# A spectral filter gated by a GEGLU block on one core: block products for slabs 12 and 13, one accumulating store, and a new opening

## The chip, the cores and the metric

The kernel runs on one core of one Trainium2 chip. Five engines take part: TensorE (PE; its weight loads are listed as PEld), VectorE (DVE), ScalarE (ACT), GpSimd (POOL) and SyncE (SP), which here issues transfers. The metric is device time in microseconds. Before the change it is 193.46 us, the median of three runs (193.43 to 193.47).

## The reference, cut to what matters

```python
x  = A_x                                  # (1, 2048, 640) bf16
xn = (x - mean(x)) / sqrt(var(x) + 1e-5)  # over the 640 columns
s  = irfft2(rfft2(xn) * (w_r + 1j * w_i)) # over rows and columns
g  = silu((gelu(xn @ w_gate) * (xn @ w_up)) @ w_down)
return x + s * g                          # w_gate, w_up: 640 x 1536; w_down: 1536 x 640
```

So two chains start from the normalized input: a two-dimensional Fourier filter and a gated feed-forward block. They meet in a product, and the input is added again.

## The kernel before, in words

The 2048 rows are held as 16 slabs of 128 rows by 640 columns (row = 16 x partition + slab), and four slabs make a group. The feed-forward block runs group by group. For each of the 12 tiles of 128 hidden columns there is a gate half (`ffn_piece` with k = 0: five matmuls into a bank psg, gelu on ACT into ge) and an up half (k = 1: five matmuls into a bank psu, a product with ge on DVE into UT). psg and psu have two banks each. Then the down projection of the group goes from UT and Wd into psg and psu again, and `gated` turns it into the gate G: a silu on ACT for groups 0, 2 and 3, a tanh on ACT and a product on DVE for group 1.

Groups 1 and 2 do the down projection with a block scheme for two slabs at a time (`product`): the two slabs and the two column halves of Wd, with the hidden tiles split into even and odd, make a 2 x 2 block product that is done in seven products of six matmuls of 320 columns rather than in eight. It needs sums of blocks of UT (`u_sum`, on DVE, into SS) and of Wd (`w_sum`, into TS), copies of partial results on ACT into snf and sums of them on DVE. Groups 0 and 3 do it plainly (`down_third`: 12 thirds of eight matmuls).

The filter runs beside it: folding of the input on DVE, two matrix stages per slab (`slab_S1`, `slab_D`), a store to DRAM and a load in another order, the product with the filter in 11 bursts (`s2_step`), a second round through DRAM, then the inverse stages per slab (`slab_S1i`, `slab_Di`) and the unfolding in groups of three slabs (`group_cs`, `group_Y`, `group_rest`). `finish` multiplies a slab by its gate, adds x and stores it: for slabs 0 to 11 a POOL transfer adds x in SBUF and SP stores, for slabs 12 to 15 DVE adds x, which `load_xt` brought.

The order is written by hand. `back` is the list of PE positions, 0 to 143: 0 to 15 are the first eight hidden tiles of group 0 in pieces, 16 to 23 its other four, 24 to 35 its down projection, and so on in 36s; 108 to 131 are the gate and up halves of group 3, 132 to 143 its down projection. `plan`, filled by `put(s, ...)`, hangs every other step behind a position. Each engine takes its instructions in the order in which they are emitted here. `gated(..., late)` with late set puts the silu behind the next piece and the product behind the one after (`put_off`, `flush`).

At the start, SP issues the loads of x (`load_x`) and of the weights (`load_w`), ACT issues those of Wg for the first six tiles. PE runs matmuls on a constant (`warm_pe`) until slab 0 is normalized (`stats`, `root_act` or `root`, `norm`) and transposed (`slab_Tparts`: chunks 0 to 2 and 3 to 4 apart, copied by DVE and by ACT).

## Time and profile before

| quantity | before |
|---|---|
| median of three runs | 193.46 us (193.43 to 193.47) |
| profiled execution | 193.65 us |
| its span, first to last instruction | 191.9 us |
| granted clock of the core | 1.000 |
| busy in the span: PE, DVE, ACT, POOL | 186.1, 150.9, 131.9, 53.9 us |
| first matmul on real data (not warm-up, not transposition) | 6.84 us |
| last matmul ends | 188.67 us |
| instructions | 4068 |

The profiled execution is one run, and its times hang together only within it; 1.75 us of its 193.65 lie outside the span. Times in rows are microseconds from the start of the span. A row of instructions reads: start, duration, engine, line, operation, what it writes and reads, count; in brackets what the engine waited for. A row of groups gives busy time and the mean of one in nanoseconds behind the bar. A row of the chain gives start, duration and work.

### The profile page before, as it was taken

The page shows a single profiled execution, that of the slowest core. Times are in us where ns is not written, and L with a number is a line of the kernel's source. Part 1 is how long each engine was busy: PE and PEld are TensorE (multiplying, and loading weights), DVE is VectorE, ACT ScalarE, POOL GpSimd, SP SyncE. Part 2 cuts the span into 40 slices and gives each one's busy share as a digit, 9 for nine tenths or more (in the row PEclk, how much of TensorE's full clock was granted, in tenths as well). Part 3 has the DMA queues.
Part 4 walks back from the last instruction along what each step waited for, and adds up shares of the span by engine and source line. Part 5 has one row for each costly group of instructions (what it writes and reads, how often), then busy time and mean ns, then how long its engine had stood idle before and what let it go on. Part 6 is the DMA issues. An engine that isn't in the chain of part 4 may idle for free.

```text
span 191.9 us, 4068 instructions
## 1 busy us (share of the span) xinstructions
PE 186.1 (97%) x1453; PEld 115.6 (60%) x1469; DVE 150.9 (79%) x364; ACT 131.9 (69%) x241; POOL 53.9 (28%) x91
## 2 busy tenths in 40 slices
PE   7999999999999999999999999999999999999993
PEld 5788854677655665566543334347775555556772
DVE  6787889899799889846978677685445898888973
ACT  4658557957878778536697878634989776876622
POOL 4458768999040200000000000002030134150400
PEclk9999999999999999999999999999999999999999
DMA  6999999948889994249996444149900084778842
GB/s 164 300 329 360 370 332 170 172 99 318 178 165 191 211 300 120 78 111 230 223 108 123 106 103 103 42 107 273 266 5 0 0 117 111 152 153 213 121 174 62
DMA packets 39700, 32.43 MB, mean 169 GB/s; under 512 B 12928, under 2 KB 37760, under 8 KB 39552
## 3 DMA queue, kind: packets, MB, share of 16 engines
q1 hardware_dynamic: 35888, 27.91, 58.6%
q0 software_dynamic: 1824, 3.28, 9.4%
q10 hardware_dynamic: 1968, 0.98, 1.9%
q8 instruction: 11, 0.18, 0.4%
q14 instruction: 9, 0.07, 0.1%
HBM read 19.03 MB, written 7.88 MB: 140 GB/s over the span
## 4 chain that ended last, share of the span: by engine, by line
PE 95%; DMA 2%; DVE 1%; issue 1%; SPq 0%; ACT 0%
PE psu L832 27%; PE psg L832 27%; PE psg L967 7%; PE psg L933 7%; PE psu L967 6%; PE psu L933 5%; PE pu L657 2%; PE pd L762 2%; PE pv L735 2%; PE pz L555 2%; PE pd L573 2%; PE px L628 2%; DMA X<-in_A_x_dram 2%; PE pt L994 1%; PE pd L575 1%
## 5 line engine op out<-in xcount | busy, mean ns | idle before, releaser
L832 PE MATMUL psu<-XG,Wu 128*128 128x512 bf16 (+2 forms) x284 | 60.4, 342 | 0.5 <-issue 0.3
L832 PE MATMUL psg<-XG,Wg 128*128 128x512 bf16 (+2 forms) x280 | 60.1, 341 | 0.6
L839 DVE TENSOR_TENSOR UT<-psu,ge 128x512 bf16<-128x512 f32 (+2 forms) x58 | 34.4, 594 | 13.6 <-PE psu L832 8.1
L837 ACT ACTIVATE ge<-psg 128x512 bf16<-128x512 f32 (+2 forms) x58 | 30.3, 523 | 21.3 <-PE psg L832 20.6
L832 PEld LDWEIGHTS <-Wu 128*128 128x128 bf16 x290 | 25.9, 98 | 20.9 <-issue 3.4
L832 PEld LDWEIGHTS <-Wg 128*128 128x128 bf16 x290 | 26.5, 98 | 18.8 <-issue 0.2
L967 PEld LDWEIGHTS <-UT 128*128 128x128 bf16 x204 | 19.1, 98 | 6.9
L813 POOL DMA_DIRECT2D VY<-in_A_x_dram x12 | 10.6, 964 | 26.2 <-ACT W L737 10.5
L713 POOL COPY vr<-VY 128x128 bf16<-128x128 bf16 x2 | 0.6, 291 | 60.2 <-DMA VY<-UDR 60.2
L644 DVE TENSOR_TENSOR RZ<-xs,W 128x960 bf16<-128x960 bf16 (+2 forms) x22 | 13.3, 647 | 4.4 <-ACT xs L640 4.4
L967 PE MATMUL psg<-Wd,UT 128*128 128x320 bf16 (+1 forms) x108 | 15.7, 290 | 0.0
L578 ACT CAST RZ<-pd 128x660 bf16<-128x660 f32 x16 | 11.3, 706 | 5.2 <-PE pd L575 5.2
L189 DVE BATCH_NORM_STATS2 st<-X 128x6 f32<-128x320 bf16 x32 | 14.0, 476 | 0.6 <-DMA X<-in_A_x_dram 0.4
L933 PEld LDWEIGHTS <-UT 128*128 128x128 bf16 x120 | 11.4, 98 | 4.8 <-issue 0.4
L967 PE MATMUL psu<-Wd,UT 128*128 128x320 bf16 (+1 forms) x96 | 13.9, 293 | 0.0
L737 ACT CAST W<-pv 128x640 bf16<-128x640 f32 x16 | 11.1, 691 | 3.1 <-PE pv L735 3.1
L763 ACT ACTIVATE W<-pd 128x640 bf16<-128x640 f32 x16 | 11.3, 706 | 1.5 <-PE pd L762 1.5
L557 ACT CAST GEN<-pz 128x640 bf16<-128x640 f32 x16 | 11.2, 698 | 1.2 <-PE pz L555 1.2
L672 ACT CAST RX<-pu 128x480 bf16<-128x480 f32 (+3 forms) x22 | 10.8, 489 | 1.1 <-DVE RX L672 0.3
L640 ACT CAST xs<-px 128x960 bf16<-128x960 f32 (+2 forms) x11 | 10.3, 933 | 0.0
L207 POOL TENSOR_TENSOR rst<-ve,mhalf 128x1 f32<-128x1 f32 (+1 forms) x6 | 5.5, 913 | 11.5 <-DVE ve L205 11.5
L933 PE MATMUL psg<-X,UT 128*128 128x320 bf16 x48 | 7.8, 300 | 0.0
(202 smaller groups left out, 302.1 us busy)
## 6 DMA issues: line engine op xcount, KB each, us to landing
ZDR<-RZ SPq DMA_DIRECT2D x16, 160.5 KB, 4.1
UDR<-RX SPq DMA_DIRECT2D x10, 240.8 KB, 3.1
B<-ZDR SPq DMA_DIRECT2D x8, 240.8 KB, 5.2
W<-UDR SPq DMA_DIRECT2D x2, 963.0 KB, 9.1
X<-in_A_x_dram SPq DMA_DIRECT2D x3, 640.0 KB, 10.3
Wd<-in_B_w_down_dram SPq DMA_DIRECT2D x1, 1920.0 KB, 14.6
VY<-in_A_x_dram POOLq DMA_DIRECT2D x12, 160.0 KB, 4.3
out_dram<-VY SPq DMA_DIRECT2D x12, 160.0 KB, 2.8
```

What stands on the lines that cost most here:

```text
L189: nc.vector.bn_stats(out=st_n[n1][:, k, :], in_=X[:, n1, 320 * k:320 * k + 320])
L557: nc.scalar.copy(out=Zt[n1], in_=pz)
L578: nc.scalar.copy(out=zd.rearrange("p c (q e) -> p c q e", e=10), in_=pd[:, :, 0:330].rearrange("p c (e q) -> p c q e", q=33))
L644: nc.vector.tensor_tensor(out=pp[-1], in0=xs, in1=WT[:, :, h0:h0 + n, l0:l0 + w], op=ALU.mult)
L672: copy(out=out, in_=src)
L737: nc.scalar.copy(out=vs, in_=pv)
L763: nc.scalar.activation(out=parts(eobuf, i, 5)[:, :, n1 - DG[i][0], :], in_=pd, func=ACT.Copy, scale=(2.0 if n1 // 4 in BY_SILU else 1.0) / ...
L832: nc.tensor.matmul(ps, lhsT=WT[:, c, t * P:(t + 1) * P], rhs=xnT[g][:, c, c0:c1_], start=(c == 0), stop=(c == 4))
L837: nc.scalar.activation(out=ges[t], in_=ps, func=ACT.Gelu_apprx_tanh)
L839: nc.vector.tensor_tensor(out=UT[:, t, c0:c1_], in0=ps, in1=ges[t], op=ALU.mult)
L933: nc.tensor.matmul(ps, lhsT=lhs[:, t, :], rhs=rhs[:, t, :], start=(t == 0 and i in (0, 1, 3)), stop=(t == 5), skip_group_check=i in (2, 4, ...
L967: nc.tensor.matmul(ph, lhsT=UT[:, t, j * P:(j + 1) * P], rhs=Wd[:, t, c0:c1_], start=(t == 0), stop=(t == NT - 1))
```

## The change: what it does

At the start: weights are loaded four tiles at a time, the first four in two parts of three and two chunks of the contraction. Wu's first load on SP stands behind a POOL write into Wu that reads a_y, and the load of slab 2 behind a POOL write that reads slab 0's statistics. The first four tiles are computed for slab 0 and then slab 1 in `ffn_quad` (four tiles of one slab share a bank, 20 matmuls of 128 columns), the others in `ffn_multi` (two tiles of two slabs share a bank). Gelu and product then work on 512 columns. The normalization and transposition of slab 0 come ahead of the second statistic of slab 1; slab 1's root moves from POOL to ACT, ahead of the table load of gelu; the second copy of the transposes of slabs 0 and 1 moves from ACT to DVE. The warm-up has 38 and 4 matmuls of 128 columns instead of 21 and 2 of 256. Statistics and constants move by some positions.

In the middle: `sb` goes from 67 to 65, so all bursts and everything counted from them, down to the unfolding, come two positions earlier.

At the end: for tiles 6 to 11 of group 3, ACT copies the up half from PSUM into UT and DVE multiplies there. Slabs 12 and 13 go through `product`, slabs 14 and 15 stay with `down_third`, in the order p0 and third (14,0), p2, p1, p4, third (14,1), p3, third (14,2), p6, p5, and the three thirds of slab 15. The last of these silus (product 5) follows its sum at once (late = 1). Slabs 12, 13 and 14 are finished whole, no longer by halves. For slab 13, x is stored to the output by SP right after its load; DVE writes the product of slab and gate over that x in SBUF, and POOL adds it to the output in DRAM with one accumulating transfer.

```diff
-    def load_w(k, t0, t1, eng=nc.sync):
+    def load_w(k, t0, t1, eng=nc.sync, c0=0, c1_=5):
         f0, f1 = t0 * P, t1 * P
-        eng.dma_start(out=(Wg, Wu)[k][:, :, f0:f1], in_=(wgv, wuv)[k][:, :, f0:f1])
+        eng.dma_start(out=(Wg, Wu)[k][:, c0:c1_, f0:f1], in_=(wgv, wuv)[k][:, c0:c1_, f0:f1])
...
     load_x(0, 1)
     load_x(1, 1)
-    load_w(1, 0, 2)
-    load_w(1, 2, 4)
-    load_x(2, 1)
-    load_w(1, 4, 6)
-    load_x(3, 1)
-    load_gu(6, 8)
-    load_x(4, 4)
-    load_gu(8, 12)
-    load_x(8, 4)
-    nc.sync.dma_start(out=Wd, in_=B_w_down.rearrange("(t p) d -> p t d", p=P))
-    load_x(12, 4)
...
     def root_act(n1):
-        rstd[n1] = c1("rst0")
+        rstd[n1] = c1("rst%d" % n1)
         nc.scalar.activation(out=rstd[n1], in_=mva[n1 // 4][:, n1 % 4, 1:2], func=ACT.Abs_reciprocal_sqrt, bias=eps)
+
+    def gelu_table():
         nc.scalar.activation(out=warm, in_=negpi, func=ACT.Gelu_apprx_tanh)
 
...
-    ones = gtile([256], BF16)
+    ones = gtile([128], BF16)
...
-    for t in (0, 2, 4):
-        load_w(0, t, t + 2, nc.scalar)
+    for part in PARTS:
+        load_w(0, 0, 4, nc.scalar, *part)
     b_0, b_1 = c1("b_0"), c1("b_1")
...
     fwd_consts()
+    nc.gpsimd.tensor_copy(out=Wu[:, 0, 0:1], in_=ab[4][0])
+    for part in PARTS:
+        load_w(1, 0, 4, nc.sync, *part)
     vt_iota(0)
-    stats(0)
+    bn_half(0, 0)
+    bn_half(0, 1)
+    bn_join(0)
+    nc.gpsimd.tensor_copy(out=X[:, 2, 0:1], in_=mva[0][:, 0, 0:1])
+    load_x(2, 1)
+    load_w(0, 4, 8)
+    load_x(3, 1)
+    load_w(1, 4, 8)
+    load_x(4, 4)
+    load_gu(8, 12)
+    load_x(8, 4)
+    nc.sync.dma_start(out=Wd, in_=B_w_down.rearrange("(t p) d -> p t d", p=P))
+    load_x(12, 4)
     bn_half(1, 0)
     root_act(0)
...
         for _ in range(n):
-            nc.tensor.matmul(warm_bank[0][:, 0:256], lhsT=ones[:, 0:P], rhs=ones, start=True, stop=True)
+            nc.tensor.matmul(warm_bank[0][:, 0:P], lhsT=ones, rhs=ones, start=True, stop=True)
...
+    XS = (13,)
...
             nc.sync.dma_start(out=t[:, a:a + w, :], in_=xv[:, 2 * pair + a:2 * pair + a + w, :])
+            for k in range(a, a + w):
+                if 2 * pair + k in XS:
+                    nc.sync.dma_start(out=outv[2 * pair + k], in_=t[:, k, :])
...
     def finish(n1):
         ks = [k for k in range(len(cut(n1)) - 1) if (n1, k) in left and (n1, k) in Gok]
-        if ("y", n1) not in done or not ks:
+        if ("y", n1) not in done or not ks or (n1 in (12,13,14) and len(ks) < 2):
             return
         sl = slice(cut(n1)[ks[0]], cut(n1)[ks[-1] + 1])
         G = Gt[n1 // 4]
         Y = st_c["Y"](n1, 1)[:, 0, sl]
-        nc.vector.tensor_tensor(out=Y, in0=Y, in1=G[:, n1 % 4, sl], op=ALU.mult)
+        out = xts[n1][:, sl] if n1 in XS else Y
+        nc.vector.tensor_tensor(out=out, in0=Y, in1=G[:, n1 % 4, sl], op=ALU.mult)
+        if n1 in XS:
+            nc.gpsimd.dma_start(out=outv[n1][:, sl], in_=out, accum_op=ALU.add)
+            left.difference_update((n1, k) for k in ks)
+            return
...
+    UP_COPY = {3: range(6, 12)}
...
         else:
-            nc.vector.tensor_tensor(out=UT[:, t, c0:c1_], in0=ps, in1=ges[t], op=ALU.mult)
-
-    def ffn_part(g, t, h):
-        for k in range(2):
-            ffn_piece(g, t, k, h * 256, h * 256 + 256)
+            ut = UT[:, t, c0:c1_]
+            if t in UP_COPY.get(g, ()):
+                nc.scalar.copy(out=ut, in_=ps)
+                ps = ut
+            nc.vector.tensor_tensor(out=ut, in0=ps, in1=ges[t], op=ALU.mult)
+
+    def ffn_quad(k, j, *part):
+        assert ("T", j) in done
+        if part[0] == 0:
+            cur["m"] = bank(k)
+        ps = cur["m"].rearrange("p (t w) -> p t w", w=P)
+        WT = (Wg, Wu)[k]
+        for a, b in [PARTS[i] for i in part]:
+            for i in range(4):
+                for c in range(a, b):
+                    nc.tensor.matmul(ps[:, i, :], lhsT=WT[:, c, i * P:(i + 1) * P],
+                                     rhs=xnT[0][:, c, j * P:(j + 1) * P], start=(i + c == 0), stop=(c == 4),
+                                     skip_group_check=True)
+        if part[-1] == 1:
+            multi_out(k, 0, ps, j * P, j * P + P)
+
+    def ffn_multi(k, t0, n, c0, c1_, half=None):
+        w = c1_ - c0
+        for j in range(c0 // P, c1_ // P):
+            assert ("T", j) in done
+        if half in (None, 0):
+            cur["m"] = bank(k)[:, 0:n * w].rearrange("p (t w) -> p t w", w=w)
+        ps = cur["m"]
+        WT = (Wg, Wu)[k]
+        for i in range(n) if half is None else range(half * n // 2, (half + 1) * n // 2):
+            for c in range(5):
+                nc.tensor.matmul(ps[:, i, :], lhsT=WT[:, c, (t0 + i) * P:(t0 + i + 1) * P], rhs=xnT[0][:, c, c0:c1_],
+                                 start=(c == 0), stop=(c == 4))
+        if half != 0:
+            multi_out(k, t0, ps, c0, c1_)
+
+    def multi_out(k, t0, ps, c0, c1_):
+        n, w = 512 // (c1_ - c0), c1_ - c0
+        flush()
+        if k == 0:
+            ge = work.tile([P, 512], BF16, tag="ge", bufs=3, name="ge")[:, 0:n * w].rearrange("p (t w) -> p t w", w=w)
+            ges[t0, c0] = ge
+            nc.scalar.activation(out=ge, in_=ps, func=ACT.Gelu_apprx_tanh)
+        else:
+            nc.vector.tensor_tensor(out=UT[:, t0:t0 + n, c0:c1_], in0=ps, in1=ges[t0, c0], op=ALU.mult)
...
-        if late:
+        if late == 1:
+            put_off.append(lambda t=one(): two(t))
+        elif late:
             put_off.append(lambda: put_off.append(lambda t=one(): two(t)))
         else:
             two(one())
...
     SS = {k: b[:, 0:2 * 6 * P].rearrange("p (i t c) -> p i t c", i=2, c=P)
-          for k, b in (((1, 0), XG[:, 0, :]), ((1, 1), RX[:, 0, :]), ((2, 0), XG[:, 0, :]), ((2, 1), SB))}
+          for k, b in (((1, 0), XG[:, 0, :]), ((1, 1), RX[:, 0, :]), ((2, 0), XG[:, 0, :]), ((2, 1), SB), ((3, 0), XG[:, 0, :]))}
...
         if at:
-            gated(g, *at, c, True)
+            gated(g, *at, c, 1 if (g, i) in ((3, 5),) else 2)
         if i == 1:
             u_sum(nc.vector, g, a, 0, 6, (3,))
-        if a == 0 and i in REST:
+        if a == 0 and i in REST and g in STR:
             u_sum(nc.vector, g, 1, TB, 6, (REST.index(i),))
...
-        for (a, b), ev in zip(PARTS, (nc.vector.tensor_copy, nc.scalar.copy)):
+        for (a, b), ev in zip(PARTS, (nc.vector.tensor_copy, nc.scalar.copy if n1 > 1 else nc.vector.tensor_copy)):
...
-    back = [(run, (ffn_slab, 0, GG), (norm_parts, 1), (slab_Tparts, 1), (vt_iota, 1), (ffn_slab, 0, UU),
-             (inv_consts, 0), (inv_consts, 1)),
-            (run, (ffn_slab, 1, GG + UU), (stats, 2), (root, 2, 1))]
-    for h in range(2):
-        for t in range(0 if h else 2, NP):
-            back.append((ffn_part, 0, t, h))
-        if h == 0:
-            back[-1] = (run, (ffn_piece, 0, NP - 1, 0, 0, 256), (slab_Tparts, 3), (ffn_piece, 0, NP - 1, 1, 0, 256))
+    back = [(run, (ffn_quad, 0, 0, 0, 1), (vt_iota, 1)),
+            (run, (ffn_quad, 1, 0, 0), (slab_Tparts, 1), (ffn_quad, 1, 0, 1)),
+            (ffn_quad, 0, 1, 0, 1),
+            (ffn_quad, 1, 1, 0, 1)]
+    for h, k, t0 in ((0, 0, 4), (0, 0, 6), (0, 1, 4), (0, 1, 6)) + tuple((1, k, t) for t in (0, 2, 4, 6) for k in range(2)):
+        back.append((ffn_multi, k, t0, 2, 256 * h, 256 * h + 256))
+    back[6] = (run, (slab_T, 2, 1), (ffn_multi, 1, 4, 2, 0, 256))
+    back[7] = (run, (slab_Tparts, 3), (ffn_multi, 1, 6, 2, 0, 256))
...
+        if g == 3:
+            items = [(product, 3, 0, i) if i < 7 else (down_third, 3) + divmod(i - 7 + 6, 3) for i in (0,7,2,1,4,8,3,9,6,5,10,11,12)]
+            back.append((run, *items[0:2]))
+            back.extend((run, it) for it in items[2:])
+            continue
...
-    put(1, inv_rest)
-    put(2, norm, 2)
-    put(3, bn_half, 3, 0)
-    put(4, bn_half, 3, 1)
-    put(4, bn_join, 3)
-    put(4, root, 3, 1)
-    put(4, slab_T, 2, 1)
-    put(5, norm, 3)
+    put(1, stats, 2)
+    put(1, root, 2, 1)
+    put(2, bn_half, 3, 0)
+    put(2, bn_half, 3, 1)
+    put(3, norm, 2)
+    put(3, bn_join, 3)
+    put(3, root, 3, 1)
+    put(3, inv_consts, 0)
+    put(3, inv_consts, 1)
+    put(4, inv_rest)
+    put(5, norm_parts, 3)
...
-    for k in range(4):
-        put(7 + 2 * k, stats, 4 + k)
-    put(13, root, 4, 4)
-    put(13, shift, 4, 4)
+    for k, at in enumerate((7, 8, 10, 12)):
+        put(at, stats, 4 + k)
+    put(12, root, 4, 4)
+    put(12, shift, 4, 4)
     for k in range(3):
         put(13, ft_phase, 1, k)
-    put(12, tinv_mask, 0)
-    put(14, tinv_mask, 1)
+    put(16, tinv_mask, 0)
+    put(18, tinv_mask, 1)
...
+    put(128, u_sum, nc.vector, 3, 0, 0, TB)
+    put(131, u_sum, nc.vector, 3, 0, TB, 6)
...
-    sb = 67
+    sb = 65
...
-    warm_pe(21)
+    warm_pe(38)
+    norm_parts(0)
+    slab_Tparts(0)
+    warm_pe(4)
     bn_half(1, 1)
     bn_join(1)
-    root(1, 1)
-    norm_parts(0)
-    slab_Tparts(0)
-    warm_pe(2)
+    root_act(1)
+    gelu_table()
+    norm_parts(1)
 
```

6 lines of the change are left out of this document (1 added, 5 removed).

## The prediction

> **What bounds the kernel now.** I read the busy lines of the page first, then the chain that ended last in order of time, then the windows.
>
> ```profile
> span 191.9 us, 4068 instructions
> PE 186.1 (97%) x1453; PEld 115.6 (60%) x1469; DVE 150.9 (79%) x364; ACT 131.9 (69%) x241; POOL 53.9 (28%) x91
> PE 95%; DMA 2%; DVE 1%; issue 1%; SPq 0%; ACT 0%
> ```
> ```profile
> 1.17 3.19 DMA X<-in_A_x_dram
> 4.38 0.90 DVE st L189 x2
> 5.70 0.30 DVE X L218
> 6.84 0.76 PE psg L832 x10
> 8.44 0.56 PE psg L832 x10
> 9.56 0.55 PE psg L832 x5
> 12.83 0.28 PE pt L543 x5
> ...
> 175.31 1.09 PE psg L967 x8
> 176.39 0.28 PE pd L762 x5
> 177.22 1.63 PE psu L967 x12
> 187.99 0.68 PE psg L967 x12
> ```
> ```profile
> 6.84:25.40 18.56, 18.56 (x196) 16.82 (x196) 15.29 (x52) 11.86 (x33) 11.55 (x18) 1.00 1.10 347
> 143.20:175.30 32.10, 31.89 (x231) 18.04 (x235) 26.86 (x48) 25.44 (x42) 8.60 (x11) 1.00 0.49 94
> 188.69:191.90 3.21, 0.00 (x0) 0.00 (x0) 0.70 (x3) 0.28 (x1) 0.00 (x0) 1.00 0.19 51
> ```
>
> The chain is TensorE (PE) for 95% of the span. The window 6.84 to 25.40 has PE busy 18.56 of 18.56 us, the long stage before the last down projection 31.89 of 32.10 (in these rows the columns are PE, PEld, DVE, ACT, POOL, clock, DMA share, GB/s). So time is gained in three ways alone: start the real matmuls before 6.84, remove matmuls, or shorten the 3.21 us after the last matmul. It is lost wherever the change makes PE wait. An instruction saved on DVE or ACT is worth nothing by itself.
>
> Unit prices of PE from the chain: 10 matmuls of 128 columns take 0.56, 5 of 256 take 0.55, 12 of 320 take 1.63 (0.136 each), a slab's five transposes 0.28.
>
> **Part 1, the start.**
>
> ```profile
> 1.18 4.55 PE L588 MATMUL psg<-GEN 128*128 128x256 bf16 x21 [1.18 <-DVE eps L229]
> 2.53 0.14 DVE L272 TENSOR_SCALAR a_y<-pb 128x1 f32<-128x1 f32 x1
> 4.29 0.29 ACT L214 ACTIVATE rst<-mva,eps 128x1 f32<-128x1 f32 x1 [2.08 <-DVE mva L195]
> 5.62 0.63 DVE L218 TENSOR_SCALAR X<-X,mva,rst 128x384 bf16<-128x384 bf16 x2
> 6.43 0.36 DVE L995 COPY XG<-pt 128x384 bf16<-128x384 bf16 x1 [0.18 <-PE pt L994]
> 11.27 0.56 POOL L207 TENSOR_TENSOR rst<-ve,mhalf 128x1 f32<-128x1 f32 x1 [1.44 <-DVE ve L205]
> 2.25:12.00 9.75, 9.40 (x93) 7.56 (x92) 7.65 (x35) 4.78 (x12) 3.94 (x8) 1.00 1.12 297
> 12.00:27.00 15.00, 14.95 (x136) 12.66 (x136) 12.96 (x38) 9.26 (x25) 10.78 (x16) 1.00 1.07 367
> ```
>
> Now the normalization of slab 0 begins at 5.62, behind both statistics of slab 1, though its root was ready at 4.29 + 0.29 = 4.58. After the change only one statistic of slab 1 (half of the 0.90) stands ahead: 4.38 + 0.45 = 4.83, 0.79 us earlier. From the start of the normalization to the first real matmul are 6.84 - 5.62 = 1.22 us, so that comes at about 6.05. The second group of the copy moves from ACT to DVE; it is needed only for the last 8 of the first 20 matmuls, 12 x 0.056 = 0.67 later, and hidden by them.
>
> The columns to the end of this stage are the same: 80 matmuls of 128 and 120 of 256 instead of 40 and 140, 4.48 + 13.2 against 2.24 + 15.4 us, equal. What the head start loses again: (a) slab 1's second statistic, its root (on ACT, 0.29) and two-part normalization run while PE does 32 matmuls of 128 (1.8 us); they need about 0.45 + 0.2 + 0.3 + 0.65 from the DVE copies on, so PE waits some 0.1. (b) ACT computes slab 1's root at about 7.3 and only then loads the gelu table (1.28) and makes the first 512-wide gelu (0.60, with a warm-up of 0.2 before it), so the first UT product (0.69; rows in part 3) starts at 9.4. Slab 2's normalization stands on DVE behind it, behind its own and slab 3's statistics (0.9 each, and 0.35 of joins) and a second UT product: 9.4 + 0.69 + 0.9 + 0.35 + 0.9 + 0.69 + 0.4 = 13.3. PE wants its transposes at 6.05 + 80 x 0.056 + 20 x 0.11 + 0.28 + 0.1 = 13.1: 0.2 lost. (c) Slab 3, with its root on POOL (0.56), 0.1. Net gain 0.79 - 0.4 = 0.4 us. Ends: 0.9 if nothing is lost and slab 1 lands sooner, -0.5 if weights are late.
>
> The weights: Wu of the first four tiles waits for a POOL copy behind a_y (2.53 + 0.14), X of slab 2 for the statistics of slab 0; on SP everything else queues behind them. Bytes in their new order until the last weight of the first half (slabs 0 and 1, four tiles of Wg and of Wu, slab 2, four more of Wg, slab 3, four more of Wu): 0.33 + 0.66 + 0.66 + 0.16 + 0.66 + 0.16 + 0.66 = 3.29 MB. The DMA moved 297 GB/s while the 512-byte rows of two-tile loads ran (2.25 to 12) and 367 when rows were 1 KB and longer. All weights are now loaded four tiles wide, 1 KB rows. So they land at 2.25 + 3.29/0.367 = 11.2, at worst at 13.3; PE needs them at 13.1 + 0.28 + 0.2 = 13.6. The first Wu part (1.38 MB) lands at 6.0 to 6.9, needed at 6.05 + 1.1 = 7.2. I take the cover as holding. The Trainium skill, page "DMA: Bandwidth & Descriptors", section "Specifications", has line rate from 512 B on; by it the longer rows bring nothing, the 13.3 holds with 0.3 to spare, and the first rival below would have 0.25 instead of 0.16. The two windows, 297 against 367, side against it.
>
> **Part 2, the middle.** The burst stage (sb 67 to 65) starts two positions earlier: two products of 0.82 sooner.
>
> ```profile
> 82.33 2.44 PE psg L933 x18
> 89.67 0.32 PE px L628 x2
> 82.94 6.26 SPq L603 DMA_DIRECT2D B<-ZDR  x10
> B<-ZDR SPq DMA_DIRECT2D x2, 240.8 KB, 3.9
> ```
>
> Its first matmul then comes after 42 product matmuls, 82.33 + 42 x 0.136 = 88.0 on the old clock; its two loads are issued at 82.94 and about 83.5 and land 3.9 later, by 87.4. Cover 0.6 us, and what follows keeps its distance; cost nothing, up to 0.5 if the cover fails. Mask and statistics that move a slot run on DVE beside a dense PE: nothing.
>
> **Part 3, the gelu products of the last group.** For tiles 6 to 11 ACT copies the up half to UT and DVE multiplies in SBUF.
>
> ```profile
> L839 DVE TENSOR_TENSOR UT<-psu,ge 128x512 bf16<-128x512 f32 x12 | 8.3, 692 | 5.0 <-PE psu L832 3.1 <-ACT ge L837 1.8
> L837 ACT ACTIVATE ge<-psg 128x512 bf16<-128x512 f32 x12 | 7.2, 600 | 3.9 <-PE psg L832 3.9
> L811 DVE TENSOR_TENSOR VY<-VY,XG 128x640 bf16<-128x640 bf16 x12 | 5.8, 481 | 0.0
> L794 DVE TENSOR_TENSOR VY<-VY,W 128x1920 bf16<-128x1920 bf16 x4 | 4.6, 1148 | 0.0
> L867 ACT ACTIVATE XG<-psg 128x320 bf16<-128x320 f32 x5 | 2.2, 432 | 1.4 <-PE psg L967 1.4
> L867 ACT ACT_TABLE_LOAD x1 | 1.3, 1283 | 0.0
> L947 DVE TENSOR_TENSOR Tfwd<-Tfwd,psu 128x320 f32<-128x320 f32 x1 | 0.5, 486 | 1.8 <-PE psu L933 1.8
> ```
>
> ACT gains 6 x 0.60 = 3.6 us in the last half of a stage where it is busy 25.44 of 32.10; 16 us of it then hold 12.7 + 3.6 at most, and the durations overlap by about 0.1 per instruction. Full, but no PE bank waits for it: two banks of each kind. DVE is relieved by 6 x (0.69 - 0.42) (0.42 between the 640 and the 320 wide bf16 products) and pays for three sums of 640 (0.48 each). Cost on PE nothing; up to 0.8 if ACT falls behind.
>
> **Part 4, the end.** Slabs 12 and 13 cost 7 x 6 = 42 matmuls of 320 instead of 48: 6 x 0.136 = 0.82 us saved. Count from T, the end of the last up matmul (175.31 now). Today's 72 matmuls, the 0.28 of the last inverse step and slab 15's last pieces end at 188.67, T + 13.36. After, the inverse step lies before T, and the matmuls alone are 12.26. Does PE wait between? The third product needs the sums over UT 10 and 11: ACT copy to T + 0.6, then DVE, behind two 0.48 and two 0.55 left over, product and two sums of 0.22, ready at about T + 2.0; PE arrives at 0.82 + 1.09 = 1.9. Wait 0.15. The DVE chain after it (0.48, 0.55, 0.56, five of 0.3, Tfwd sum 0.49, 0.55, 1.15, three of 0.25, Y0 sum) reaches the Y0 sum at T + 7.6; the product that overwrites that bank comes at T + 8.3. ACT, with the table load and four silus of 0.43, frees the bank for slab 15 at T + 8.9, wanted at T + 9.1. So no further wait, but with 0.2 to 0.7 us of cover only. Net 0.82 - 0.15 = 0.67. Ends: 0.82, and -0.4 if DVE comes 1 us later than I count.
>
> The store of slab 13's x stands on SP behind its own load and ahead of stores of VY slabs and the loads of slabs 14 and 15.
>
> ```profile
> 172.95 0.98 SPq L728 DMA_DIRECT2D RX<-in_A_x_dram  x2
> ```
>
> Those loads are issued at 172.95 today and first read about T + 8.5 = 183.8, so 5 us of delay there are free. Slabs 12 and 14 are finished whole rather than by halves; their work is done before slab 15's last pieces. The 3.21 us behind the last matmul stay: slab 15's last piece is as before.
>
> **Sum.** The profiled execution took 193.65 us, 0.19 over the median. 193.65 - 0.4 - 0.67 = 192.58; from the median 193.46 the same gives 192.4.
>
> **Rivals.** R1, the head start is eaten (weights or the DVE order of slabs 1 to 3): 193.46 - 0.67 = 192.8. For it: 0.3 to 2 us of DMA cover; against: SP and ACT queues share the load. R2, the end is eaten by DVE and ACT, whose covers of 0.2 to 0.7 fail by 0.7: 193.46 - 0.4 = 193.1. R3, the other side: the accumulating store of slab 13 ends the kernel.
>
> ```profile
> DMA to landing us min/median/max: 3.3/4.3/4.9
> DMA to landing us min/median/max: 3.6/5.6/9.5
> ```
>
> The first row is POOL's accumulating transfers into SBUF (L813), the second the slowest loads (L603). The store is issued when slab 13's product is done, about T + 9.5, POOL being idle; the kernel ends at T + 12.4 + 3.2 = 15.6. It decides from a landing of 6.1 us on and makes the kernel slower than before from 7.2; at 9.5, 195.8. Against: 4.9 is the largest seen, and nothing queues behind it; for: none into DRAM is seen. R4, the clock: the warm-up row shows 21 matmuls of 256 columns in 4.55 us, 0.217 each, twice the 0.11 of later; full speed came near 5.2, 4.0 us after the first one. The new warm-up (38 of 128 columns, 0.108 each, 4.1 us) ends about there and real work begins right behind it. If the short pause before the transposes starts those 4.0 us anew, work runs at half speed until 9.2 and costs up to 2.0: between 192.4 and 194.4, middle 193.4. Against: three runs within 0.04 us show no wandering clock. The Trainium skill, page "TensorE: Matmul & The Clock Gate", section "Part 1: The HAM clock gate", calls the activity window (3.4 us) free-running; by that rule the switch could fall up to 8.0 and cost 1.4. R5, it does nothing, gains and waits cancelling: 193.4.
>
> **Chances.** Forecast 0.49 (own range 191.9 to 192.8), R1 0.16, R2 0.10, R3 0.05, R4 0.10, R5 0.05, other PE waits that make it slower 0.05. A change of 0.2% (0.39 us) is what can be told. Faster: forecast, R1, a third of R2 and of R4, 0.71; same: R5, most of R2, a third of R4, 0.13; slower: R3, a third of R4, the last, and what I can't name, 0.16. The range 191.6 (just under both gains at their upper ends, 193.46 - 0.9 - 0.82 = 191.7) to 193.7 (R1, R2, R5 and the better half of R4) leaves out R3 and the worst.
>
> **What would show it.** First real matmul near 6.05 and the 512-wide ones at 25.0 instead of 25.40; PE dense at 82 to 95; 12.4 us from T to the last matmul; the accumulating store landing before the last SP store. Wrong: PE idle on Wg or Wu before 14 us, psg waiting for ACT behind T, warm-up matmuls at 0.107 beyond 5.3, or the last landing on POOL's queue.

## The result and the profile after

The changed kernel takes 194.09 us (median of 17 runs, 193.65 to 195.96) against 193.67 us for the kernel before (17 runs on the same chips, 193.42 to 194.04): ratio 1.0032, 95% interval 1.0018 to 1.0047. It is slower by 0.2 to 0.5%, where the prediction had it faster by 0.5%; 194.09 lies above the top of its range, 193.7. The profiled execution took 193.99 us, its span is 192.2 us.

The chain that ended last in the profile after (start, duration, work), at its start, at its only new stall and at the end:

```profile
1.17 3.73 DMA X<-in_A_x_dram
4.92 0.49 DVE st L180
5.41 0.29 DVE X L211
5.75 0.71 PE pt L1047 x5
...
14.05 0.60 ACT ge L899
14.65 0.38 ACT GEN L369
15.03 0.59 ACT XG L555
15.67 0.27 PE pt L1047 x2
...
175.86 0.81 PE psg L993 x6
...
187.45 0.68 PE psg L1027 x12
188.15 0.29 ACT XG L925
```

TensorE over time in the profile after (start, duration, engine, line, work, count, in brackets the idle time before it):

```profile
1.04 4.24 PE L596 MATMUL psg<-GEN 128*128 128x128 bf16 x38 [1.04 <-DVE eps L222]
5.75 0.71 PE L1047 MATMUL pt<-ident,X 128*128 128x128 bf16 x5 [0.47 <-DVE X L211]
6.70 1.46 PE L872 MATMUL psg<-XG,Wg 128*128 128x128 bf16 x20
7.99 0.83 PE L872 MATMUL psu<-XG,Wu 128*128 128x128 bf16 x12
```

And two windows, the opening and what lies behind the last matmul, first of the profile before, then of the one after (columns: PE, PEld, DVE, ACT, POOL, clock, DMA share, GB/s):

```profile
6.84:25.24 18.40, 18.40 (x196) 16.73 (x196) 15.13 (x52) 11.83 (x33) 11.43 (x17) 1.00 1.10 347
188.67:191.90 3.23, 0.00 (x0) 0.00 (x0) 0.71 (x3) 0.28 (x1) 0.00 (x0) 1.00 0.18 51
```
```profile
6.70:25.60 18.90, 18.79 (x217) 17.29 (x216) 14.79 (x46) 11.70 (x25) 13.13 (x21) 1.00 1.06 368
188.13:192.20 4.07, 0.00 (x0) 0.00 (x0) 0.71 (x3) 0.28 (x1) 0.00 (x0) 0.90 0.51 116
```

Here 25.24 and 25.60 are where a row of 512-wide matmuls first appears; the prediction's 25.40 is the same place in the chain, where the changed kernel has 25.76. From these rows the span's 0.3 us follow:

| stretch | before | after | difference |
|---|---|---|---|
| to the first 512-wide matmul | 25.24 | 25.60 | +0.36 |
| from there to T, the end of the last up matmul (175.31, 175.86) | 150.07 | 150.26 | +0.19, of which 0.28 is the inverse step that moved ahead of T |
| T to the end of the last matmul (188.67, 188.13) | 13.36 | 12.27 | -1.09, of which 0.28 the same step |
| behind the last matmul | 3.23 | 4.07 | +0.84 |

The opening was to win 0.4 and lost 0.36. Within it, the start is 0.14 earlier (6.84 to 6.70); the first 20 matmuls take 7.99 - 6.70 = 1.29 us where 20 at full speed take 1.11, so the clock was still low at their start (the transposes at 5.75 take 0.71, where five take 0.54 at full speed); and the second transposes of slab 3 wait for ScalarE, about 0.3. T to the last matmul is what was forecast. The tail, the time behind the last matmul, was to stay and grew by 0.84. The opening is one profile's: two other profiles of the same opening, start_only and after_noacc below, reach the 512-wide matmuls at 25.68 and 25.13.

### The profile page after: what moved, and what is told of

Same layout as the page of the kernel before. It is cut to its first block, busy times and chain, and to the rows that moved or that the text cites. A ratio compares the mean times of both kernels' runs of the same rounds, so it can differ in the third digit from the quotient of the medians.

```text
span 192.2 us, 4113 instructions
## 1 busy us (share of the span) xinstructions
PE 185.4 (96%) x1486; PEld 117.2 (61%) x1502; DVE 151.9 (79%) x363; ACT 134.3 (70%) x239; POOL 53.0 (28%) x93
## 3 DMA queue, kind: packets, MB, share of 16 engines
q0 software_dynamic: 1968, 3.45, 9.9%
## 4 chain that ended last, share of the span: by engine, by line
PE 93%; DMA 2%; ACT 1%; issue 1%; DVE 1%; SPq 0%
PE psu L850 23%; PE psg L850 22%; PE psg L993 9%; PE psu L993 6%; PE psg L1027 5%; PE psu L1027 5%; PE psg L888 3%; PE psu L888 3%; PE pu L665 2%; PE pv L747 2%; PE pd L774 2%; PE pz L563 2%; PE pd L581 2%; DMA X<-in_A_x_dram 2%; PE px L636 2%; PE psg L872 1%
## 5 line engine op out<-in xcount | busy, mean ns | idle before, releaser
L850 PE MATMUL psu<-XG,Wu 128*128 128x512 bf16 x194 | 49.0, 379 | 0.5 <-issue 0.3
L850 PE MATMUL psg<-XG,Wg 128*128 128x512 bf16 x190 | 48.7, 379 | 0.5
L855 ACT ACTIVATE ge<-psg 128x512 bf16<-128x512 f32 x40 | 23.9, 598 | 16.4 <-PE psg L850 15.6
L861 DVE TENSOR_TENSOR UT<-psu,ge 128x512 bf16<-128x512 f32 x34 | 23.3, 685 | 9.2 <-PE psu L850 5.5
L850 PEld LDWEIGHTS <-Wu 128*128 128x128 bf16 x200 | 18.0, 98 | 20.2 <-issue 3.2
L850 PEld LDWEIGHTS <-Wg 128*128 128x128 bf16 x200 | 18.6, 98 | 18.0
L652 DVE TENSOR_TENSOR RZ<-xs,W 128x960 bf16<-128x960 bf16 (+2 forms) x22 | 13.3, 647 | 2.9 <-ACT xs L648 2.5
L586 ACT CAST RZ<-pd 128x660 bf16<-128x660 f32 x16 | 11.3, 706 | 5.2 <-PE pd L583 5.2
L1027 PE MATMUL psg<-Wd,UT 128*128 128x320 bf16 (+1 forms) x84 | 12.1, 288 | 0.0
L1027 PE MATMUL psu<-Wd,UT 128*128 128x320 bf16 (+1 forms) x72 | 10.4, 290 | 0.0
L993 PE MATMUL psg<-X,UT 128*128 128x320 bf16 x60 | 9.8, 300 | 0.0
L993 PE MATMUL psu<-Wd,UT 128*128 128x320 bf16 x60 | 9.8, 299 | 0.0
```

Of the source, the lines that this page charges most:

```text
L586: nc.scalar.copy(out=zd.rearrange("p c (q e) -> p c q e", e=10), in_=pd[:, :, 0:330].rearrange("p c (e q) -> p c q e", q=33))
L652: nc.vector.tensor_tensor(out=pp[-1], in0=xs, in1=WT[:, :, h0:h0 + n, l0:l0 + w], op=ALU.mult)
L850: nc.tensor.matmul(ps, lhsT=WT[:, c, t * P:(t + 1) * P], rhs=xnT[g][:, c, c0:c1_], start=(c == 0), stop=(c == 4))
L855: nc.scalar.activation(out=ges[t], in_=ps, func=ACT.Gelu_apprx_tanh)
L861: nc.vector.tensor_tensor(out=ut, in0=ps, in1=ges[t], op=ALU.mult)
L993: nc.tensor.matmul(ps, lhsT=lhs[:, t, :], rhs=rhs[:, t, :], start=(t == 0 and i in (0, 1, 3)), stop=(t == 5), skip_group_check=i in (2, 4, ...
```

## The experiments

Times are medians; the kernel before, run beside each group of them, had 193.51 to 193.69. "Opening" is the change's start up to the 512-wide matmuls, "end" is group 3's down projection, slab 13's store, the ScalarE copies and sb = 65.

**The two halves apart.** `start_only` has the new opening with the old end and sb = 67. `end_only` has the old opening with the new end and sb = 65.

> The new opening alone; the bursts and the last group as before. Theory A (the opening costs what the changed kernel's trace shows, 26.03 against 25.67 us at the first 512-wide matmul): 0.3 to 0.5 us slower than before, first 512-wide matmul near 26.0. Rival B (the clock of TensorE comes late in some executions, because warm-up ends before the switch): the median is near before, and single executions stand 1 to 2 us above it. Rival C (the opening is neutral and the loss sits in the end): within 0.1 us of before.

> The old opening with the new bursts' place and the new end. Theory A (the end saves 0.8 us on TensorE and gives it back behind the last matmul): within 0.15 us of before, last matmul 0.8 us earlier against the same point, 4.1 us from the last matmul to the end of the span instead of 3.2. Rival C (all the loss is in the end): 0.3 us slower or more.

start_only took 194.70 us (7 runs, 193.74 to 195.69; ratio 1.0059, 1.0029 to 1.0089). end_only took 193.15 us (12 runs, 192.99 to 193.37; ratio 0.9970, 0.9960 to 0.9981). Neither is where theory A had it: the opening costs more than 0.5 us, the end gains more than 0.15. So the whole loss comes with the opening, about 1 us with a wide scatter (three of the seven executions are at 195.3 or more, as rival B has it, while the profiled one, at 194.31, reaches the 512-wide matmuls 0.44 us late, nearly as A has it), and the end gains 0.5 us of the 0.67 forecast. In end_only's profile the matmuls from T to the last take 12.26 us and 3.8 us lie behind them, so the missing part is in the tail.

**The accumulating store.** Two kernels add slab 13 on VectorE and store it with SP, one on the old opening, one on the new.

```diff
-    XS = (13,)
+    XS = ()
```

> As the run before, but slab 13 is finished like slab 12: VectorE adds x, SyncE stores. Theory A1 (the accumulating transfer into DRAM, 3.4 us with its reads, slows the last stores): 0.5 to 0.8 us faster than before, 3.2 to 3.5 us behind the last matmul. Rival A2 (it is the bunching of the stores of slabs 12 and 13 with slab 15's, whichever way they are made): 0 to 0.2 us faster than before, 3.8 to 4.1 us behind the last matmul.

> The changed kernel without the accumulating transfer. Theory A with A1: 0.2 to 0.4 us faster than before; with A2: 0.2 to 0.4 us slower, like the changed kernel. Rival B: executions 1 to 2 us above the others remain, since the opening is the new one.

end_noacc: 193.01 us (7 runs; ratio 0.9970, 0.9951 to 0.9988). after_noacc: 194.00 us (12 runs; ratio 1.0025, 1.0006 to 1.0044). The first is as A1 has it (0.64 us faster than before, 3.5 us behind the last matmul), the second is slower than before, as A2 has it. A third pair comes below: mended_noacc is 0.47 us faster than mended. The medians thus fall by 0.14, 0.09 and 0.47; the first two alone are hardly more than can be told. The profiles agree better. The tail is 3.8 us with the transfer and 3.5 without on the old opening, 4.1 and 3.8 on the new one, in both pairs. Issues between 188 and the end, with KB and time to landing, with the transfer (after) and without (after_noacc; end_noacc has the same three rows):

```profile
out_dram<-X SPq DMA_DIRECT2D x1, 80.0 KB, 2.6
out_dram<-X SPq DMA_DIRECT2D x1, 48.0 KB, 2.3
out_dram<-X SPq DMA_DIRECT2D x1, 32.0 KB, 1.9
```
```profile
out_dram<-X SPq DMA_DIRECT2D x1, 80.0 KB, 1.6
out_dram<-X SPq DMA_DIRECT2D x1, 48.0 KB, 1.6
out_dram<-X SPq DMA_DIRECT2D x1, 32.0 KB, 1.5
```

The transfer itself lands in 3.4 us (3.6 in end_only) and is never the last, but slab 15's pieces, in flight beside it, take 0.4 to 1.0 us longer to land. Without it VectorE has one more sum of 640 (0.49) ahead of slab 15's pieces and ends 0.1 later (188.64 against 188.54, end_noacc and end_only). That takes back part of the gain; about 0.3 us is left in each pair of profiles.

**The ScalarE copies of the last group** (on the old opening):

```diff
-    UP_COPY = {3: range(6, 12)}
+    UP_COPY = {}
```

> The old opening with the new end, without the ScalarE copies of the up half for tiles 6 to 11 of the last group. If these copies only save VectorE time that nobody waits for, the time is that of the new end with them, 193.0 to 193.3. If they are what lets the sums over UT and slab 12's and 13's products be ready in time, TensorE waits in the end for 0.3 to 0.8 us and the time is 193.4 to 194.0.

193.50 us (12 runs; ratio 0.9999, 0.9987 to 1.0012), against 193.15 with the copies (0.35 us by these medians, 0.48 when each is set against the kernel before of its own group). Without them the whole gain of the end is gone. It does not go where the expectation had it: TensorE still ends its last matmul at 187.81 (187.71 with them) without a wait, and that 0.10 is the opening's (512-wide matmuls at 25.30 and 25.20). The chain at the end runs over VectorE instead of TensorE; the row is the share by line from 175 to 189, here without the copies, then with them:

```profile
by line: DVE X L816 11.9%; issue 11.5%; ACT XG L881 9.2%; DVE X L798 7.6%; DVE Tfwd L963 6.9%; DVE X L824 6.5%; DVE VY L816 6.2%; DVE W L790 6.2%; DVE W L772 5.4%; DVE X L782 4.9%; DVE UT L853 4.4%; DVE UT L923 4.3%; DVE X L780 4.2%; DVE Y 
```
```profile
by line: PE psg L983 28.2%; PE psg L949 23.3%; PE psu L983 18.7%; PE psu L949 17.5%; PE psu L842 4.6%; ACT XG L881 2.0%; DVE X L816 1.7%; DVE X L824 1.6%; issue 0.5%
```

VectorE ends 0.1 us later in that profile, and the last store, the last of four that SP issues one after the other, goes out at 188.84 instead of 188.57. So the two profiles, 0.3 us apart, differ by 0.1 in the opening and by 0.2 behind the last matmul; what else the medians differ by is in no profile.

**TensorE's clock.** Longer and shorter warm-up in the changed kernel:

```diff
-    warm_pe(38)
+    warm_pe(46)   # warm_more
+    warm_pe(24)   # warm_less
```

> The changed kernel with 46 warm-up matmuls instead of 38, so that TensorE goes from the warm-up into slab 0's transposes without the idle 0.47 us that the profile of the changed kernel has at 5.28. If the clock theory is right (the switch to full speed falls out when TensorE idles in the opening, and falls late in the executions at 195 and above), no execution is above 194.6 and the median is 193.7 to 194.0. If the warm-up's idle time has nothing to do with it, the median is 194.1 as the changed kernel's (or up to 0.3 more, where the longer warm-up delays the transposes), and one execution in six is still above 194.9.

> The changed kernel with 24 warm-up matmuls instead of 38: TensorE is then idle from 3.7 to about 5.8 us in every execution. If an idle TensorE in the opening sends its clock back to half speed, or never lets it up (as in the one profile at 196.0, where 1.79 us of idle time stood ahead of 3.7 us at half speed), most executions are at 194.9 to 196.5, and the profile shows quad matmuls at about 0.11 us instead of 0.056 until 7 us or later. If the late executions have another cause, the median stays at 194.1 with one in six above 194.9.

warm_more: 194.32 us (11 runs, 193.93 to 196.31; ratio 1.0040). It did not help, and one execution was still at 196.3, against the expectation: without any pause before the transposes the clock came up at 6.4 in its profile. The transposes start at 5.98 instead of 5.75, mostly because slab 1's x landed later there (statistic at 5.15 instead of 4.92). warm_less: 195.28 us (6 runs, 194.84 to 196.27; ratio 1.0096, 1.0071 to 1.0121): all six executions are at 194.8 or more, as the clock theory has it. Its profile, of a 196.26 execution, has TensorE idle for 2.22 us and then at half speed up to 11.4 us:

```profile
6.00 0.72 PE L1047 MATMUL pt<-ident,X 128*128 128x128 bf16 x5 [2.22 <-DVE X L211]
6.96 2.33 PE L872 MATMUL psg<-XG,Wg 128*128 128x128 bf16 x20
9.07 1.49 PE L872 MATMUL psu<-XG,Wu 128*128 128x128 bf16 x12
```

**What makes slab 1's x land late.** It lands at 4.92 instead of 4.38, and the normalization of slab 0 stands behind its first statistic. Three edits of the changed kernel: Wg's first loads in rows of 512 bytes again, Wg's issue 0.13 us later again (through the memset ahead of eps), and Wu's first loads ahead of the POOL copy:

```diff
-    for part in PARTS:                      # rows_512
-        load_w(0, 0, 4, nc.scalar, *part)
+    for t in (0, 2):
+        load_w(0, t, t + 2, nc.scalar)
...
-    ones = gtile([128], BF16)               # ones_256 (the warm-up reads ones[:, 0:P])
+    ones = gtile([256], BF16)
...
+    for part in PARTS:                      # wu_early: moved to behind load_x(1, 1)
+        load_w(1, 0, 4, nc.sync, *part)
-    nc.gpsimd.tensor_copy(out=Wu[:, 0, 0:1], in_=ab[4][0])
```

> The changed kernel with the first four tiles of Wg loaded by two transfers of 512-byte rows (all five chunks, two tiles each) instead of two of 1,024-byte rows. If the longer rows take the DMA engines away from slab 1's x, whose landing went from 4.38 to 4.92 us, the statistics of slab 1 start at about 4.4 again, the first matmul on Wg at about 6.3 instead of 6.74, and the time is 193.6 to 193.8, unless Wg is then late and TensorE waits for it. If slab 1 lands when it does for another reason (the load issues and their order), the statistics stay at 4.9 or within its scatter (4.8 to 5.1 in the three profiles of this opening) and the time stays at 194.1.

> The changed kernel with the 256-wide memset of ones that the kernel before had (the warm-up still reads 128 of them). It puts eps back from 0.99 to about 1.13 us, and with it ScalarE's first issue of Wg from 1.06 to 1.19 us, as before. If slab 1's x lands late because Wg's descriptors now enter the DMA engines ahead of it, slab 1's statistics start at 4.2 to 4.5 again (4.8 to 5.6 in the seven profiles of the new opening), the first matmul on Wg comes at about 6.2, and the time is 193.5 to 193.8. If 0.14 us of issue time do not matter, the statistics stay at 4.8 or later and the time at 194.0 to 194.2.

> The changed kernel with the two first Wu loads issued on SyncE's queue right behind slab 1's x (at 1.6 us, as the kernel before did) and no longer behind the GpSimd copy (2.95 us). If slab 1's x lands late because its queue runs empty behind it and so gets a smaller share of the engines than ScalarE's queue, the statistics of slab 1 start at 4.2 to 4.5 again and the time is 193.5 to 193.8. If more transfers in flight only slow slab 1 further, they start at 5.0 or later, and the time is 194.1 to 194.5.

rows_512: 193.90 us (13 runs, 193.58 to 196.01; ratio 1.0013, 0.9994 to 1.0032); in its profile, which is of the 196.01 execution, slab 1's statistics start at 5.61: the length of the rows is not the cause. wu_early: 193.99 us (12 runs, 193.59 to 194.37; ratio 1.0013, 1.0000 to 1.0026), statistics at 5.16: an empty queue is not it either. ones_256: 193.91 us (12 runs, 193.30 to 194.32; ratio 1.0010, 0.9995 to 1.0025), statistics at 4.11, without a wait, and no execution above 194.4. VectorE and TensorE in ones_256:

```profile
4.11 0.44 DVE L180 BATCH_NORM_STATS2 st<-X 128x6 f32<-128x320 bf16 x1
1.18 4.23 PE L596 MATMUL psg<-GEN 128*128 128x128 bf16 x38 [1.18 <-DVE eps L222]
5.21 0.74 PE L1047 MATMUL pt<-ident,X 128*128 128x128 bf16 x5
6.18 1.60 PE L872 MATMUL psg<-XG,Wg 128*128 128x128 bf16 x20
```

The first real matmul is at 6.18, near the 6.05 of the prediction. Eps is ready 0.14 us later with the wide memset, ScalarE's table instruction waits for eps, and Wg's loads stand behind that. So the edit turns round which load is issued first, ScalarE's of Wg or SP's of slab 1's x. The two issues, in the profile after and then in ones_256:

```profile
1.06 0.47 ACTq L88 DMA_DIRECT2D Wg<-in_B_w_gate_dram  x1
1.17 0.42 SPq L84 DMA_DIRECT2D X<-in_A_x_dram  x1
```
```profile
1.19 0.44 ACTq L88 DMA_DIRECT2D Wg<-in_B_w_gate_dram  x1
1.17 0.42 SPq L84 DMA_DIRECT2D X<-in_A_x_dram  x1
```

The three kernels below that carry the same edit have the statistics at 4.15, 4.17 and 4.58; the ten profiles without it in which VectorE waits for slab 1 are all at 4.78 or later. That the order of these two issues is the link was not tried in another way. But the time falls by only 0.2: in this profile the clock came up at 6.8 us, so the transposes and the first six of the 20 matmuls ran at half speed, and the 20 took 1.43 us.

**ScalarE's order in front of slab 3's second transposes.** psB has two buffers, so these transposes wait for the copy of slab 2's, which stands behind a gelu and a constant (L369). First all ten constants three steps later, then one only, behind the copy:

```diff
-        put(3 + g, ft_v, g)                 # consts_late
-        put(8 + g, ft_v, 5 + g)
+        put(6 + g, ft_v, g)
+        put(11 + g, ft_v, 5 + g)
...
-        put(3 + g, ft_v, g)                 # const_behind
+        put(6 if g == 2 else 3 + g, ft_v, g)
```

> The changed kernel with the ten ScalarE instructions that build the constants of the forward tables put three steps later, and what reads them two or three steps later, so that ScalarE copies slab 2's transposes out of PSUM right behind one gelu. If the order of ScalarE's queue is what holds slab 3's second transposes (TensorE's wait at 15.03 to 15.67 in the changed kernel), that wait shrinks by 0.4 to 0.5 us, the 512-wide matmuls start at about 25.4 instead of 25.8, and the time is 193.6 to 193.7. If the wait is only moved (to the gelu in front, or to a later step where the constants stand now), the time stays at 194.0 to 194.2.

> The changed kernel with one ScalarE instruction moved: the third constant of the forward tables goes behind the copy of slab 2's transposes instead of ahead of it. Nothing on GpSimd moves. If that instruction stands in the way of slab 3's second transposes, TensorE's wait at 15.03 to 15.67 shrinks by 0.35 to 0.45 us, the later start of the tables that took the gain away with all ten constants does not occur, and the time is 193.6 to 193.8. If the gain is given back here too, the loss lies in the order of the constants as such and the time is 194.0 to 194.3.

consts_late: 194.49 us (12 runs; ratio 1.0060, 1.0035 to 1.0085). The opening does end 0.48 earlier, at 25.12, but the tables and statistics that use the constants come late: at the first pz matmul (a matrix stage of the filter) its lead is down to 41.84 - 41.73 = 0.11 us, and the first matmul of the next down projection comes at 82.77 instead of 82.54, behind the changed kernel. const_behind: 193.86 us (12 runs, 193.34 to 195.28; ratio 1.0011, 0.9990 to 1.0032). From the first 256-wide matmul to the one behind slab 3's second transposes it takes 15.29 - 11.36 = 3.93 us where the changed kernel takes 15.78 - 11.67 = 4.11: the edit is worth 0.2 us, and its profile shows no later wait that takes them back.

**Slab 0 without slab 1.** The first statistic of slab 1 behind slab 0's normalization:

```diff
     load_x(12, 4)
-    bn_half(1, 0)
     root_act(0)
...
     norm_parts(0)
+    bn_half(1, 0)
     slab_Tparts(0)
```

> The changed kernel with slab 1's first statistic put behind slab 0's normalization in VectorE's order, so that the first real matmul no longer waits for slab 1's landing whatever sets that. The root of slab 0 is there at about 4.6, the normalization starts at 4.6 to 4.7 instead of 5.33, the first statistic of slab 1 then stands ahead of the copies (until 5.4 to 5.7), and the first matmul on Wg comes at 5.9 to 6.2 instead of 6.74. If slab 1's landing in front of slab 0 is what costs the opening, the time is 193.3 to 193.6, and the executions at 195 and more are gone, as TensorE no longer idles between warm-up and transposes. If half of the head start goes to the clock, which in the profiles so far came up anywhere from 3.9 to 7.1 us, the time is 193.6 to 193.9.

193.92 us (12 runs, 193.37 to 194.67; ratio 1.0009, 0.9995 to 1.0023). The first real matmul comes at 5.90, 0.8 earlier than in the changed kernel, and the late executions are gone; yet the 512-wide matmuls come at 25.55. New waits, for weights, take the gain. In TensorE's rows:

```profile
5.90 1.28 PE L871 MATMUL psg<-XG,Wg 128*128 128x128 bf16 x20
11.33 2.36 PE L887 MATMUL psg<-XG,Wg 128*128 128x256 bf16 x20 [0.44 <-DMA Wg<-in_B_w_gate_dram]
14.34 1.27 PE L887 MATMUL psu<-XG,Wu 128*128 128x256 bf16 x10 [0.24 <-DMA Wu<-in_B_w_up_dram]
```

**The edits together.** `all_three` is warm_more, rows_512 and consts_late. `mended` is ones_256 and const_behind, `mended_noacc` the same with XS = (). `later_loads` is mended_noacc with x of slabs 4 to 15, the last Wg and Wu tiles and Wd held back:

```diff
     bn_join(1)
+    nc.gpsimd.tensor_copy(out=X[:, 4, 0:1], in_=mva[0][:, 1, 0:1])
+    load_x(4, 4)                            # moved here with all loads behind it
     root_act(1)
```

> The three edits together: longer warm-up, 512-byte rows for the first four tiles of Wg, constants later. If the three are separate causes that add up, the 512-wide matmuls start at about 25.0 as the prediction had it, and the time is 192.9 to 193.3, with no execution above 194. If one of them carries all, the time is that of the best single edit, about 193.7.

> The changed kernel with both single edits that helped the opening: the 256-wide memset of ones (Wg issued at 1.19 us) and the third constant behind slab 2's copy. If the two are separate, slab 0's transposes start at 5.2 and slab 3's second ones wait no more; the opening then ends 0.3 to 0.5 us earlier than with either alone, at 24.8 to 25.0, and the time is 193.3 to 193.5. If the clock (full speed from 3.9 to 7.1 us, wherever it falls) and the arrival of the weights now set the opening, it ends at 25.1 to 25.3 as with either alone, and the time is 193.6 to 193.8.

> The same with slab 13 added on VectorE and stored by SyncE, no accumulating transfer. If that transfer keeps the DMA engines busy beside slab 15's last stores, the last store of 32 KB lands in 1.5 us instead of 1.9 to 2.0, the tail behind the last matmul is 3.4 to 3.8 us instead of 4.1, VectorE ends about 0.1 us later, and the time is 0.2 to 0.4 us below the run with it (192.9 to 193.4). If the tail is only that of bunched stores, there is no difference over 0.1.

> The mended kernel without the accumulating transfer (193.76 us), with all loads behind the last Wu of the opening (x of slabs 4 to 15, tiles 8 to 11 of Wg and Wu, Wd) held until slab 1's statistics, by a GpSimd copy that waits for them: they are issued from about 6.6 to 7 us on instead of from 6.5 at the earliest. If those loads, in flight beside the weights, make them late (0.7 us of waiting for the first Wu part or the second Wg part in the two mended profiles), that wait goes, the opening ends at 24.8 to 25.1, and the time is 192.8 to 193.2. If the weights are late because the engines are simply full with what is ahead of them in the queue, the wait stays at 0.4 to 0.8 us, and the time is 193.6 to 193.9.

all_three: 194.94 us (6 runs; ratio 1.0066, 1.0041 to 1.0091), with the loss of consts_late in it. mended: 194.23 us (12 runs; ratio 1.0034, 1.0021 to 1.0048). mended_noacc: 193.76 us (12 runs; ratio 1.0015, 1.0005 to 1.0025), 0.47 us below mended, of which its tail of 3.8 instead of 4.1 us is 0.3, as its first theory has it. The edits to the opening do not add up. mended begins its real matmuls at 5.79, earlier than the prediction, and its clock is up at 4.6, so neither the start nor the clock is left; the opening still ends at 25.72. TensorE's waits in mended (us in total, times, longest):

```profile
PE psg L888 <- DMA Wg<-in_B_w_gate_dram: 0.7, 1, 0.7
PE psu L872 <- DMA Wu<-in_B_w_up_dram: 0.2, 1, 0.2
```

and the chain that leads to the first of them:

```profile
4.84 6.93 DMA Wg<-in_B_w_gate_dram
```

Wg's second four tiles, the fifth entry in the prediction's list of bytes, land at 11.77. What had been moved by then, in mended (columns as in the windows above):

```profile
0.00:11.77 11.77, 9.71 (x132) 9.09 (x132) 8.06 (x44) 5.03 (x9) 4.44 (x16) 1.00 0.86 279
```

That is 11.77 us at 279 GB/s, 3.28 MB, where the list up to this load has 2.47 MB: 0.8 MB of what stands behind it had been moved beside it. In mended_noacc it is Wu's first part that lands late, and TensorE waits 0.70 us for it. later_loads: 193.83 us (12 runs, 192.97 to 194.64; ratio 1.0016, 0.9998 to 1.0033). In its profile, of a 193.28 execution, Wg's second part is in time, but Wu's first part still lands at 7.66 and costs 0.26 us; its median is no better. So holding the later loads back does not mend it; as their issue moved only from 6.34 to 7.24 us, what part they have in it stays open.

Of all versions the old opening with the new end is the best: end_noacc at 193.01 and end_only at 193.15 us beat both kernels.

## Why the prediction was wrong

**Part 1 failed**, in four of its steps.

"4.38 + 0.45 = 4.83" took slab 1's landing from the trace of before, as if the new opening could not move it. It moved to 4.92, and between 4.78 and 5.61 in the other profiles without the wide memset. A one-line detail of the diff, ones at 128 instead of 256, did it; the way, through eps and the order of issue on ScalarE and SP, is read from the traces and was not tried apart. This ate the start: 6.70 instead of 6.05.

The losses (a) to (c), 0.4 in all, followed VectorE and the roots. What came was none of them but the copy of slab 2 on ScalarE, which the prediction did not set against two transposition buffers; const_behind gives 0.2 for it, the trace about 0.3. With these numbers the profile adds up: 0.65 for the start, 0.18 for the clock and 0.28 for ScalarE, less the 0.4 of losses that did not come, are 0.71 of the 0.76 us by which the 512-wide matmuls come later than forecast (25.76 instead of 25.0).

R4, the clock, had a chance of 0.10, against it "three runs within 0.04 us show no wandering clock". The clock does wander. A matmul of 128 columns starts every 0.107 us at half speed and every 0.056 at full speed; by this spacing full speed came at 3.8 (after_noacc, rows_512), 4.6 (mended), 5.1 (all_three), 6.4 (warm_more), 6.8 (ones_256) and 7.1 us (after). Nor did it come "near 5.2" in the kernel before: 21 matmuls in 4.55 us, 0.217 each, leave no faster ones among them. The kernel before starts real work at 6.84 and so hardly feels it; real work at 6.0 runs partly at half speed. The rival's form was right in part: a pause can put full speed off and cost up to 2 us (the profiles of rows_512 and warm_less at 196 us show it), but warm_more, without a pause, came up late as well. Its place in the chances was too low: three of the changed kernel's 17 executions and three of the 7 of start_only are at 194.9 or more. That these, too, are late by the clock is likely; none of them was profiled. The Trainium skill, page "TensorE: Matmul & The Clock Gate", section "Part 1: The HAM clock gate", calls the activity window free-running, 3.4 us long; the switches spread over 3.8 to 7.1 us agree with that.

"I take the cover as holding": in the changed kernel itself TensorE waits for no weights. With the first real matmul at 5.8 to 6.2 us they bind in four of five profiles (mended, mended_noacc, norm_first and later_loads, not ones_256). In these four Wu's first part lands at 6.9 to 8.0 us; the prediction has 6.0 to 6.9. Wg's second part lands at 11.3 (norm_first) and 11.8 (mended) where TensorE waits for it; the list of bytes, at 367 GB/s in order of issue, gives 2.25 + 2.47/0.367 = 9.0. The last weight of the list lands at 14.3 in norm_first, later than the 13.3 called the worst. The list took loads as landing one after the other; mended shows 0.8 MB of later ones moved beside this one, and from 2.25 to 11.77 us 338 GB/s instead of 367. Why the landings differ from execution to execution stays open. R1, the head start eaten, is thus what remains when the rest is mended; the opening ended at 25.1 to 25.7 in every profile but the two where the clock fell back or came very late (rows_512, warm_less).

**Part 2** was right: from the 512-wide matmuls to T there is no new wait, and the stretch is 0.09 us shorter without the moved step.

**Part 3** came out better than "cost on PE nothing", and for a reason that the prediction gave no price: without the copies the chain that ends last runs over VectorE. They carry 0.35 to 0.5 us by the medians, of which the profiles show 0.2, behind the last matmul.

**Part 4** was right on TensorE: 0.81 saved against 0.82, no wait where 0.15 was allowed, 12.27 us from T against 12.4. It failed with "the 3.21 us behind the last matmul stay". They became 4.07. Three parts can be read off the profiles. Without the accumulating transfer and on the old opening the tail is 3.45 (end_noacc, 191.2 - 187.75): VectorE ends 0.89 behind the last matmul instead of 0.82, and the last store lands in 1.5 instead of 1.4 us. Then about 0.3 more (after_noacc: 191.8 - 188.0 = 3.8) in all kernels with new opening and new end; it lies behind the last landing (190.5 in after_noacc, 1.3 us from the end, against 0.9 to 1.0 in end_noacc). SP's waits in its last lines have one row for TensorE's sequencer, here of end_noacc, then of the profile after:

```profile
SPq L1199 <- PEq L1199: 0.6, 2, 0.5
```
```profile
SPq L1241 <- PEq L1241: 0.9, 2, 0.7
SPq L1241 <- DMA out_dram<-X: 0.6, 2, 0.4
SPq L1241 <- DMA out_dram<-RX: 0.5, 1, 0.5
```

In the last four microseconds the profile after also has a transfer of instructions, which end_noacc's lacks. The link between the two is argued and was not tried. The rest, about 0.3, is the accumulating transfer, which R3 had in another form: it does not end the kernel, it slows the stores that do.

## What to carry to other kernels

When one opening replaces another, take no arrival time over from the old trace: check what each load's issue waits for, down to the constant that the queue's first instruction needs, and which of two queues issues first, and count a weight as there only when the engines could have moved everything in flight. A head start is worth only as much as the next limit leaves: here slab 1's x, ScalarE's order, the clock and the weights lay within 0.5 us of each other, and mending one exposed the next. At the end of a kernel, price the time behind the last matmul anew whenever stores move together, and test the halves of a change apart, since one of them may be worth keeping.

## What the runs showed of the hardware

Full speed of TensorE is lost after far less than a whole window of idle time. In the 196.01 execution of rows_512 the clock was up at 3.8 us, TensorE then idled for 1.79 us, and from about 7 to 10.7 us it ran at half speed. Windows of that profile (columns as above; the clock is the one behind POOL):

```profile
2.50:3.50 1.00, 1.00 (x13) 1.00 (x11) 0.53 (x5) 0.00 (x0) 0.77 (x2) 1.00 0.79 198
3.50:4.50 1.00, 1.00 (x17) 0.97 (x15) 0.74 (x3) 0.19 (x1) 0.53 (x2) 1.00 1.03 332
4.65:6.44 1.79, 0.00 (x0) 0.00 (x1) 0.83 (x3) 0.00 (x0) 0.00 (x0) 1.00 1.11 335
7.50:8.50 1.00, 1.00 (x12) 1.00 (x11) 0.60 (x3) 0.43 (x2) 0.00 (x0) 0.50 1.03 323
9.50:10.50 1.00, 1.00 (x13) 1.00 (x11) 0.00 (x0) 0.84 (x3) 1.00 (x4) 0.50 1.09 365
11.00:12.00 1.00, 1.00 (x21) 0.99 (x19) 0.92 (x3) 0.00 (x0) 0.00 (x0) 1.00 1.12 370
```

The count behind TensorE's busy time is of matmuls at work: twelve or thirteen in a microsecond at a clock of 0.50, and 21 at full speed in the last row. In the first row, in the warm-up, it is thirteen too, yet the clock column reads 1.00: the first switch has to be read from the matmuls. In after_noacc a pause of 0.99 us at the same clock had no such effect. The same section of the Trainium skill has the default speed return after an idle window of about 3.4 us; here 1.79 us were enough. The times at which the clock changed in that profile, 3.8, about 7.1 and 10.7, are 3.2 to 3.7 us apart, and TensorE was idle for about half of the first stretch; it looks as if a share of each window, and not the whole of it, had to be busy. One profile shows it; it was not tried further.

An accumulating transfer of 160 KB into DRAM landed in 3.4 to 3.6 us where a plain store takes about 1.8, and with it in flight a store of 32 KB took 1.9 to 2.0 us instead of 1.5.
